# Softmax denominators from four tiles instead of seven, with VectorE adding the first four exponential tiles, and v in three buffers instead of four

## The chip, the cores and the metric

The kernel runs on one core of one Trainium2 chip. The metric is the device time of one execution in microseconds (us), as the median of several runs. Times inside an execution come from a profile of one execution, counted from the start of its span.

The engines are named as the profile names them: PE is TensorE, PEld its weight loads, DVE is VectorE, ACT is ScalarE, POOL is GpSimd, SP is SyncE, which issues DMAs. PSUM is the memory that TensorE writes its sums to; SBUF is the working memory of all engines.

## The reference

An attention over 8 batches, 12 heads, 448 positions and a head size of 64, with q and k normalised, followed by two dense layers with a leaky ReLU between them:

```python
def rmsnorm(x, g):
    return x / np.sqrt(np.mean(x * x, axis=-1, keepdims=True) + 1e-06) * g

q_n, k_n = rmsnorm(q, g_q), rmsnorm(k, g_k)
scores = np.matmul(q_n, k_n.transpose(0, 1, 3, 2)) / np.sqrt(64)
attn = np.exp(scores - scores.max(-1, keepdims=True))
attn = attn / (attn.sum(-1, keepdims=True) + 1e-09)
x = np.matmul(attn, v)                       # (8, 12, 448, 64)
x = x.transpose(0, 2, 1, 3).reshape(3584, 768)
h = x @ w_in                                 # 768 -> 2048
out = np.maximum(0.01 * h, h) @ w_out        # 2048 -> 768
```

The change concerns `attn.sum`, the softmax denominator.

## The kernel before

**Units and tiles.** The attention is cut into 24 units; a unit is four heads of one batch, so a batch has three units (`NQ` is 3). The 448 key positions of a unit are cut into 7 tiles (`NS` is 7) of 64. For tile t, `score` (L195) makes the scores of 64 keys against all 448 queries for the four heads: PSUM tile `sT`, 128 partitions (two heads' keys) by 2 x 448 (two head pairs, index a). `ex` (L214, ScalarE) writes their exponentials to `et[:, t]` in f16, 128 x 896. The sum of `attn.sum` runs over the keys, so over the partitions of each half and over the seven tiles; it is done by matmuls with ones.

**The loop.** From L928 on, unit u is done in one turn of four steps d = 0 to 3, with score tiles (0), (1, 2), (3, 4), (5, 6) (`STEPS`). Instructions are issued in the order in which they stand; each engine executes its own in that order. In step 0, after the scores of tile 0 of unit u, come the leftovers of unit u-1:

- `shift_max(u)` (L232, L234): VectorE takes the maximum over tile 0 and multiplies it into an identity, giving `dg`.
- `pv_slot(u-1)` (L341): TensorE multiplies all seven exponential tiles with v, 28 matmuls of 448 columns.
- `zcol(u-1)` (L283): TensorE sums the exponentials with `onesr`, 16 matmuls on four strips of 32 columns: tiles (0, 1), (6), (2, 3), (4, 5) for each half of the queries (y) and head pair (a). Units 4 to 22 take this path (`narrow`).
- `shift_mm(u)` (L244, L245, L253): TensorE multiplies `dg` with ones, so that the maximum reaches every partition; VectorE reduces it to the bias `eb` of the exponentials of unit u. The matmul comes straight behind `zcol` on TensorE.
- `pv_out(u-1)` (L295) on ScalarE and `zcol_sum(u-1)` (L300) on VectorE clear the two results out of PSUM; `zcol_inv` (L305, L306) forms the reciprocals and copies them by DMA to tile `rz`; `xmul_pool` or `xmul_sb` (L321) multiplies, on POOL or VectorE, into `xts`.

Units 0 to 3 and unit 23 take the older path: `zsum` (L265), 28 matmuls of 448 columns over all seven tiles, and `zinv`.

**What fills the steps.** After its scores and exponentials, each step calls `fill`. It takes items from `queue`: matmul groups of the two dense layers of an earlier batch, which are queued when a batch's units are done: `moe1` (L363), `moe2` (L404), `seven` (L445, a product with seven block multiplications in place of eight, whose extra sums L426 to L435 and PSUM evictions L452, L461 are VectorE's) and in the last batches `late1` (L565). How many items a step takes is worked out from costs written in the code. Behind each item one of the step's `jobs` is issued; what is left of the jobs follows after the last item. An item's evictions are held in `pend` and issued by `flush`, ahead of the next item's matmuls or at the end of the items.

The jobs of a turn prepare later units on VectorE, ScalarE and SP. Step 1: `prep_g(u+1)` (L151), `prep_ssq(u+2)` (L155, two reductions). Step 2: `prep_rinv(u+2)` (L160, L161, ScalarE), `prep_norm(u+2)` (L167, two VectorE products which wait for it), `prep_trd(u+2)` (a transposing DMA on SP, which waits for these). Step 3: `prep_sq(u+3)` (L144, ScalarE).

**v.** `load_v(u)` (L124) is a DMA on POOL's queue into one of `NV` fixed buffers, unit u into buffer u mod `NV`; it waits until the `pv` that read the buffer before has ended. With `NV` 4, the loop issues `load_v(u+3)` in step 0 of turn u.

**Buffers.** `zpool` holds one buffer of each of its tiles (`x32`, `zs`, `rz`), `epool` two of `et`. PSUM has four banks of tag `aux`, which the items, `zcol` and others share, and two double banks `sT`, which the scores and `pv` share.

Of the kernel before, what the change touches and what calls it, by code (L numbers as in the profile page):

```python
# [9 lines left out]
FP16 = mybir.dt.float16  # L10
AF = mybir.ActivationFunctionType
ALU = mybir.AluOpType
# [6 lines left out]
def kernel(  # L19
# [11 lines left out]
    nc = tc.nc  # L31

    B, H, S, D = q.shape
    QH = 4
    NS = 7
    P = 128
    NQ = H // QH
    NU = B * NQ
# [1 line left out]
    KT = DM // P  # L40
    FT = DF // P
    DELTA = 1.0
    NV = 4

    cst = ctx.enter_context(tc.tile_pool(name="cst", bufs=1))
    raws = ctx.enter_context(tc.tile_pool(name="raws", bufs=3))
# [3 lines left out]
    zpool = ctx.enter_context(tc.tile_pool(name="zpool", bufs=1))  # L50
# [6 lines left out]
    def aux(shape, dtype, name):  # L57
        if held:
            return held[0].pop(0)
        return psum.tile(shape, dtype, tag="aux", bufs=4, name=name)  # L60
# [14 lines left out]
    onesr = cst.tile([P, 32], FP16)  # L75
# [12 lines left out]
    gate_t = cst.tile([P, 1], FP16)  # L88
    vts = [cst.tile([P, 2, NS, D], FP16, name=f"vt{i}") for i in range(NV)]
    win16 = cst.tile([P, NQ, 2, DF], FP16)  # L90
# [20 lines left out]
    st = {}  # L111

    def rows(x, u):
        b, g = divmod(u, NQ)
        return x[b, QH * g:QH * g + QH].rearrange("(a r) (p t) d -> (r p) a (t d)", r=2, t=NS)

    def load(u, engines=None):
        raw[u] = [raws.tile([P, 2, NS, D], FP32, tag=name, name=name) for name in ("rq", "rk")]
        st[u] = {}
        for t, src, eng in zip(raw[u], (q, k), engines or (nc.sync, nc.sync)):  # L120
            eng.dma_start(t.rearrange("p a t d -> p a (t d)"), rows(src, u))

    def load_v(u):
        nc.gpsimd.dma_start(vts[u % NV].rearrange("p a t d -> p a (t d)"), rows(v, u))  # L124

# [8 lines left out]
    def buf(u, name):  # L134
        if name not in st[u]:
            shape, dtype, bufs = SHAPES[name]
            st[u][name] = prep_p.tile(shape, dtype, tag=name[:2] if bufs == 3 and name != "qkT" else name, bufs=bufs, name=name)
        return st[u][name]
# [7 lines left out]
    def prep_sqp(u, tis=BOTH):  # L146
        for ti in tis:
            nc.gpsimd.tensor_tensor(buf(u, f"sq{ti}"), raw[u][ti], raw[u][ti], op=ALU.mult)
# [49 lines left out]
    def qk(u, steps):  # L198
        st[u]["sT"] = []
        for t in steps:  # L200
            sT = slot()
            score(u, t, (sT[:, 0], sT[:, 1]))
            st[u]["sT"].append((t, sT))
# [51 lines left out]
    def gate(u):  # L255
        nc.gpsimd.tensor_copy(gate_t, buf(u, "n16")[:, 1, NS - 1, 1, D - 1:D])

    xts = {}

    def zsum(u, t0=0, t1=NS):  # L260
        s = st[u]
        for t in range(t0, t1):
            for r in range(2):
                for a in range(2):
                    nc.tensor.matmul(s["zt"][r][64 * a:64 * a + 64, 0:S], ones16[64 * r:64 * r + 64],  # L265
                                     s["et"][64 * r:64 * r + 64, t, a], start=(t == 0), stop=(t == NS - 1))

    def zsum_slot(u):
        s = st[u]
# [4 lines left out]
    HS = S // 2  # L274

    def zcol(u):
        s = st[u]
        s["zc"] = aux([P, 512], FP32, "zc")
        for i, (t, n) in enumerate(((0, 2), (NS - 1, 1), (2, 2), (4, 2))):
            for y in range(2):  # L280
                for a in range(2):
                    c = 32 * (2 * y + a)
                    nc.tensor.matmul(s["zc"][c:c + 32, 0:n * HS].rearrange("p (k x) -> p k x", k=n), onesr,  # L283
                                     s["et"][:, t:t + n, a, HS * y:HS * y + HS], start=(i == 0), stop=(i == 3))

    def pv_slot(u):
        s = st[u]
        s["pslot"] = slot()
        s["pv"] = [s["pslot"][:, r] for r in range(2)]
        pv(u)  # L290

    def pv_out(u):
        s = st[u]
        s["x32"] = zpool.tile([P, 2, S], FP32, tag="x32", name="x32")
        nc.scalar.copy(s["x32"], s["pslot"][:, :, 0:S])  # L295

    def zcol_sum(u):
        s = st[u]
        s["zs"] = zpool.tile([P, HS], FP32, tag="zs", name="zs")
        nc.vector.tensor_reduce(s["zs"], s["zc"][:, 0:S].rearrange("p (k x) -> p x k", k=2), axis=AXL.X, op=ALU.add)  # L300
        drop(s["zc"])
# [11 lines left out]
    def xmul_sb(u):  # L313
        xmul_pool(u, nc.vector)
# [19 lines left out]
    def pv(u, t0=0, t1=NS):  # L334
# [3 lines left out]
        for t in range(t0, t1):  # L338
            for r in range(2):
                for a in range(2):  # L340
                    nc.tensor.matmul(s["pv"][r][64 * a:64 * a + 64, 0:S], vts[u % NV][64 * r:64 * r + 64, a, t],  # L341
                                     s["et"][64 * r:64 * r + 64, t, a], start=(t == 0), stop=(t == NS - 1))
# [354 lines left out]
    def narrow(u):  # L697
        return 4 <= u < NU - 1
# [46 lines left out]
    with tc.manual_schedule():  # L745
# [108 lines left out]
        load_v(3)  # L854
        load(5)
        prep_sqp(4, (0,))
        load_v(4)
        for f in range(2):
            load_w_out(8 * f, 8)
        qk(1, (2,))  # L860
# [26 lines left out]
        prep_norm(3)  # L887
        load(6)
        gate(3)
        prep_sqp(4, (1,))  # L890
        prep_sqp(5)
        load_v(5)
        qk(2, (2,))
        ex(2)
        trn(3, 0, vcopy)
# [32 lines left out]
        for u in range(3, NU):  # L928
            for d in range(4):
                if d > 0 or u > 3:  # L930
                    qk(u, STEPS[d])
                    if d == 0:
                        shift_max(u)
                        if u == 6:
                            xmul_sb(u - 2)
                        if narrow(u - 1):
                            pv_slot(u - 1)
                            zcol(u - 1)
                            shift_mm(u)
                            pv_out(u - 1)  # L940
                            zcol_sum(u - 1)
                        else:
                            zsum_slot(u - 1)
                            pv(u - 1)
                            shift_mm(u)
                            zinv(u - 1)
                    ex(u)
                jobs = []

                def job(fn, *args):  # L950
                    jobs.append(lambda: fn(*args))

                if d == 0:
                    if u == 3:
                        prep_norm(4)
                        gate(4)
                    elif narrow(u - 1):
                        if u < NU - 1:
                            job(zcol_inv, u - 1)
                    else:  # L960
                        xmul(u - 1)
                    if u + 4 < NU:
                        job(load, u + 4)
                    if u + 3 < NU:
                        load_v(u + 3)
                    if u < 6:
                        prep_sqp(u + 3)
                if d == 1 and narrow(u - 1) and not 5 <= u < 8 and u < NU - 1:
                    xmul_pool(u - 1)
                if u == NU - 1:  # L970
                    if d == 1:
                        job(zcol_inv, u - 1)
                    if d == 2:
                        xmul_pool(u - 1)
                if fed(u, d) and u > 3:
                    push(u // NQ - 1)
                if (u, d) in ((3, 1), (4, 0)):
                    for ti in range(2):
                        prep_tr(u + 1, ti, VV)
                if d == 1 and 5 <= u < NU - 1:  # L980
                    job(prep_g, u + 1)
                if u + 2 < NU:
                    if d == 1:
                        for ti in range(2):
                            job(prep_ssq, u + 2, ALL, (ti,))
                    if d == 2:
                        job(prep_rinv, u + 2)
                        for ti in range(2):
                            job(prep_norm, u + 2, ALL, (ti,))
                        if u > 3:  # L990
                            job(prep_trd, u + 2)
                if d == 1 and 4 <= u < 8:
                    job(weight_sum, u - 4, 0)
                if d == 0 and 5 <= u < 9:
                    job(weight_sum, u - 5, 1)
                if d == 2 and 6 <= u < 8:
                    job(xmul_sb, u - 1)
                if u == NU - 2 and d == 0:
                    for n, tile_ in ((1, (raws, "rq", 3)), (2, (raws, "rk", 3)), (3, None), (4, (prep_p, "sq", 3))):
                        job(win_sum, n, 1, tile_)  # L1000
                    for n in (3, 1, 2, 4):
                        job(x_sum, LATE, n)
                if d == 3 and 6 <= u < NU - 3:
                    for ti in range(2):
                        job(prep_sq, u + 3, ALL, (ti,))
                fill(u, d, jobs)
# [4 lines left out]
        for i, ns in enumerate(((3, 1), (2, 4))):  # L1011
            c, fn = queue[i]
# [33 lines left out]
```

## Time and profile before

| | us |
|---|---|
| median of 3 runs (lowest, highest) | 421.58 (420.45, 421.69) |
| the profiled execution | 420.8 |
| its span in the profile | 419.0 |
| VectorE: `tensor_tensor` 128x512 f16 (L426), mean | 0.42 |
| VectorE: `tensor_tensor` 128x1024 f16 (L426), mean | 0.68 |
| VectorE: `tensor_reduce` 128x896 f32 from PSUM (L232), mean | 1.09 |
| VectorE: norm 128x896 (L167), mean | 1.07 |
| POOL: L321, mean | 2.08 |
| PE: waits for ACT `et` in L195, sum | 3.6 |

Lines of the profile give a start, a duration, the engine, the line of the kernel, the operation with its tiles (out<-in) and how many were merged into one row (x16). A bracket at the end is the idle time of the engine just ahead, and what ended it. Durations of TensorE's matmuls overlap one another; distances between their starts are the better measure. A turn of the loop takes about 12.5 to 19 us, and TensorE is the engine with the least free time.

### The profile page before, as it was taken

To read this page: it belongs to the slowest core of one execution; us is meant where nothing else is said; L and a number is where in the kernel's file an instruction comes from. 1 tells how busy PE (TensorE), PEld (TensorE's weight loads), DVE (VectorE), ACT (ScalarE), POOL (GpSimd) and SP (SyncE) were. 2 spreads that over 40 slices of the span, in tenths; PEclk is the share of its full clock that TensorE was granted. 3 is DMA by queue.
4 is the path that set the end of the run, shared out by engine and by line. 5 is a ranking of instruction groups with operands and counts; after the bars stand their busy time and mean duration, and the time that the engine had idled before them with its cause. 6 is when DMAs were issued, how large, how long until landed. Compare 5 with 4: busy or idle time off the path is not lost.

```text
span 419.0 us, 9148 instructions
## 1 busy us (share of the span) xinstructions
PE 402.7 (96%) x3731; PEld 217.6 (52%) x3731; DVE 279.5 (67%) x459; ACT 304.6 (73%) x474; POOL 82.9 (20%) x75
## 2 busy tenths in 40 slices
PE   7787999999999999999999999999999999999995
PEld 7454444544445544454445544454445547558863
DVE  5888675898569736576449746468349788627762
ACT  5999877768887689867986779967986657653600
POOL 1958422200010121210121111120101101010000
PEclk9999999999999999999999999999999999999999
DMA  8999996889664996677665796578554460032023
GB/s 265 239 251 260 237 252 85 219 153 207 163 153 74 216 229 108 166 177 165 158 127 105 201 193 154 152 147 186 159 111 45 119 152 13 2 82 76 2 54 97
DMA packets 71949, 62.39 MB, mean 149 GB/s; under 512 B 36324, under 2 KB 67044, under 8 KB 71908
## 3 DMA queue, kind: packets, MB, share of 16 engines
q1 hardware_dynamic: 61312, 49.62, 47.2%
q0 software_dynamic: 10272, 11.80, 18.1%
q8 instruction: 29, 0.48, 0.4%
q10 hardware_dynamic: 324, 0.39, 0.3%
q14 instruction: 12, 0.10, 0.1%
HBM read 45.61 MB, written 11.01 MB: 135 GB/s over the span
## 4 chain that ended last, share of the span: by engine, by line
PE 83%; ACT 9%; DVE 6%; issue 1%; DVEq 0%; ACTq 0%
PE hps L363 27%; PE sT L195 8%; PE sT L341 6%; ACT et L214 6%; PE ma L445 5%; PE md L445 5%; PE mc L445 5%; PE bank L445 5%; PE bank L565 4%; PE op L404 3%; PE zc L283 3%; PE mb L445 3%; PE warm L743 2%; PE sT L445 2%; DVE n L167 1%
## 5 line engine op out<-in xcount | busy, mean ns | idle before, releaser
L214 ACT ACTIVATE et<-sT,eb 128x896 f16<-128x896 f32 x166 | 159.5, 1010 | 17.9 <-PE sT L195 16.3
L363 PE MATMUL hps<-xt,win 128*128 128x448 f16 x600 | 120.8, 353 | 0.2 <-DVE xt L350 0.2
L363 PEld LDWEIGHTS <-win 128*128 128x128 f16 x612 | 56.8, 98 | 58.2 <-issue 9.7
L321 POOL TENSOR_TENSOR xt<-x,rz 128x896 f16<-128x896 f32 x16 | 33.2, 2076 | 148.5 <-DMA rz<-zs 117.7
L167 DVE TENSOR_TENSOR n<-rq,rinv 128x896 f16<-128x896 f32 (+2 forms) x25 | 26.7, 1069 | 52.2 <-ACT rinv L161 49.4
L195 PE MATMUL sT<-qkT 64*64 64x448 f16 x664 | 52.4, 363 | 4.7 <-ACT et L214 3.6
L357 ACT ACTIVATE gt<-hps 128x448 f16<-128x448 f32 x100 | 52.4, 549 | 5.4 <-PE hps L363 5.1
L155 DVE TENSOR_REDUCE ssq<-sq 128x14 f32<-128x896 f32 (+2 forms) x49 | 50.3, 1057 | 0.7 <-ACT sq L144 0.7
L445 PEld LDWEIGHTS <-sa 128*128 128x128 f16 x352 | 32.8, 98 | 26.3 <-issue 6.1
L295 ACT COPY x<-sT 128x896 f32<-128x896 f32 x19 | 17.2, 907 | 36.1 <-DVE sT L245 36.1
L124 POOL DMA_DIRECT2D vt<-in_v_dram x24 | 18.2, 758 | 114.5 <-PE sT L341 107.1
L195 PEld LDWEIGHTS <-qkT 64*64 64x64 f16 x672 | 15.5, 104 | 38.0 <-issue 34.6
L445 PEld LDWEIGHTS <-gt 128*128 128x128 f16 x264 | 25.2, 98 | 18.7 <-issue 2.1
L341 PE MATMUL sT<-et,vt 64*64 64x448 f16 x532 | 28.5, 349 | 0.3
L404 PE MATMUL op<-wout,gt 128*128 128x384 f16 x160 | 28.4, 327 | 0.0
L232 DVE TENSOR_REDUCE sT<-sT 128x1 f32<-128x896 f32 x22 | 24.1, 1093 | 5.1 <-PE sT L195 4.9
L341 PEld LDWEIGHTS <-vt 64*64 64x64 f16 x672 | 20.7, 107 | 11.3 <-issue 1.7
L167 DVE TENSOR_TENSOR n<-rk,rinv 128x896 f16<-128x896 f32 (+2 forms) x26 | 26.1, 1010 | 0.0
L404 PEld LDWEIGHTS <-gt 128*128 128x128 f16 x192 | 17.6, 98 | 14.0 <-issue 2.9
L445 PE MATMUL ma<-wout,gt 128*128 128x384 f16 x128 | 23.5, 326 | 0.0
L426 DVE TENSOR_TENSOR sa<-gt 128x512 f16<-128x512 f16 (+1 forms) x15 | 8.1, 542 | 16.0 <-ACT gt L357 12.1
L144 ACT ACTIVATE sq<-rq 128x896 f32<-128x896 f32 (+2 forms) x18 | 16.3, 913 | 1.1 <-DMA rq<-in_q_dram 1.1
(136 smaller groups left out, 522.5 us busy)
## 6 DMA issues: line engine op xcount, KB each, us to landing
rq<-in_q_dram SPq DMA_DIRECT2D x24, 448.0 KB, 4.1
rk<-in_k_dram SPq DMA_DIRECT2D x24, 448.0 KB, 5.6
out_dram<-ost SPq DMA_DIRECT2D x52, 192.0 KB, 2.9
rz<-zs SPq DMA_DIRECT2D x76, 112.0 KB, 2.3
vt<-in_v_dram POOLq DMA_DIRECT2D x24, 224.0 KB, 5.5
win<-in_moe_w_in_dram POOLq DMA_DIRECT2D x8, 384.0 KB, 12.4
wout<-in_moe_w_out_dram POOLq DMA_DIRECT2D x2, 1536.0 KB, 25.6
out_dram<-ost SPq DMA_DIRECT2D x4, 96.0 KB, 2.1
```

Of the source, the lines that this page charges most:

```text
L124: nc.gpsimd.dma_start(vts[u % NV].rearrange("p a t d -> p a (t d)"), rows(v, u))
L155: nc.vector.tensor_reduce(buf(u, "ssq")[:, ti, :, c[0]:c[1]], buf(u, f"sq{ti}")[:, :, c[0]:c[1]], axis=AXL.X, op=ALU.add)
L167: nc.vector.tensor_tensor(buf(u, "n16")[:, ti, c[0]:c[1]].rearrange("p s a d -> p a s d"), src[:, :, c[0]:c[1]], buf(u, "rinv")[:, ti, :, ...
L195: nc.tensor.matmul(banks[a][64 * r:64 * r + 64, 0:S].rearrange("p (t x) -> p t x", t=NS), kT(u, r, a, t), qT(u, r, a), start=True, stop=True)
L214: nc.scalar.activation(s["et"][:, t], sT[:, :, 0:S], AF.Exp, bias=s["eb"], scale=1.0)
L232: nc.vector.tensor_reduce(s["spare"][:, 511:512], sT[:, :, 0:S], axis=AXL.XY, op=ALU.max)
L321: eng.tensor_tensor(xts[b][:, g], s["x32"], s["rz"], op=ALU.mult)
L341: nc.tensor.matmul(s["pv"][r][64 * a:64 * a + 64, 0:S], vts[u % NV][64 * r:64 * r + 64, a, t], s["et"][64 * r:64 * r + 64, t, a], start=(t ...
L357: nc.scalar.activation(dst, src, AF.Prelu, bias=0.0, scale=1.0, alpha=0.01)
L363: nc.tensor.matmul(hps[:, 0:S], win16[:, kt // 2, kt % 2, ts(ft, P)], xt[:, kt // 2, kt % 2], start=(kt == 0), stop=(kt == KT - 1))
L404: nc.tensor.matmul(op2[:, 0:HC], gt[:, ft, ds(col(t), P)], wout16[:, ft, ds(HC * half, HC)], start=(ft == 0), stop=(ft == FT - 1))
L445: nc.tensor.matmul(bank[:, 0:HC], a[:, f], b[:, f], start=(first and f == 0), stop=(f == HF - 1), skip_group_check=not first)
```

## The change

- `acc(u, t)` is new: VectorE adds exponential tile t to a running f16 sum `ea` (128 x 2 x 448, one buffer in `zpool`). The first call (t = 1) adds tiles 0 and 1, the next two add tiles 2 and 3.
- The calls are jobs: t = 1 and t = 2 in step 2, after `prep_rinv` and ahead of `prep_norm`; t = 3 in step 3, ahead of `prep_sq`. Units 4 to 23 have them.
- `zcol` multiplies tiles 4 and 5, then 6, then `ea`: four matmuls each, of 448, 224 and 224 columns, twelve in place of sixteen. Tile 6 goes into one half of the columns and `ea` into the other.
- `zsum` takes `ea` and tiles 4, 5, 6 where a unit has `ea`; among the units of that path, this is unit 23.
- `NV` is 3. The loop issues `load_v(u+2)` in place of `load_v(u+3)`. Ahead of the loop, `load_v(4)` moves from behind `prep_sqp(4, (0,))` to behind `gate(3)`, and `load_v(5)` leaves that part.

```diff
-    NV = 4
+    NV = 3
...
+    NA = 4
+
+    def acc(u, t):
+        s = st[u]
+        if "ea" not in s:
+            s["ea"] = zpool.tile([P, 2, S], FP16, tag="ea", name="ea")
+        nc.vector.tensor_tensor(s["ea"], s["et"][:, 0] if t == 1 else s["ea"], s["et"][:, t], op=ALU.add)
+
+    def ztile(u, t):
+        s = st[u]
+        return s["ea"] if "ea" in s and t < NA else s["et"][:, t]
+
     def zsum(u, t0=0, t1=NS):
         s = st[u]
+        if "ea" in s:
+            t0 = max(t0, NA - 1)
         for t in range(t0, t1):
+            e = ztile(u, t)
...
-                                     s["et"][64 * r:64 * r + 64, t, a], start=(t == 0), stop=(t == NS - 1))
+                                     e[64 * r:64 * r + 64, a], start=(t == 0 or e is s.get("ea")), stop=(t == NS - 1))
...
     def zcol(u):
         s = st[u]
         s["zc"] = aux([P, 512], FP32, "zc")
-        for i, (t, n) in enumerate(((0, 2), (NS - 1, 1), (2, 2), (4, 2))):
+        for k, t in ((-1, NA), (0, NS - 1), (1, 0)):
             for y in range(2):
                 for a in range(2):
                     c = 32 * (2 * y + a)
-                    nc.tensor.matmul(s["zc"][c:c + 32, 0:n * HS].rearrange("p (k x) -> p k x", k=n), onesr,
-                                     s["et"][:, t:t + n, a, HS * y:HS * y + HS], start=(i == 0), stop=(i == 3))
+                    q = slice(HS * y, HS * y + HS)
+                    if k < 0:
+                        nc.tensor.matmul(s["zc"][c:c + 32, 0:S].rearrange("p (k x) -> p k x", k=2), onesr,
+                                         s["et"][:, t:t + 2, a, q], start=True, stop=True, skip_group_check=True)
+                    else:
+                        nc.tensor.matmul(s["zc"][c:c + 32, HS * k:HS * k + HS], onesr, ztile(u, t)[:, a, q],
+                                         start=False, stop=True, skip_group_check=True)
...
         prep_sqp(4, (0,))
-        load_v(4)
...
         gate(3)
+        load_v(4)
         prep_sqp(4, (1,))
         prep_sqp(5)
-        load_v(5)
...
-                    if u + 3 < NU:
-                        load_v(u + 3)
+                    if u + 2 < NU:
+                        load_v(u + 2)
...
                     if d == 2:
                         job(prep_rinv, u + 2)
+                        if u >= 4:
+                            job(acc, u, 1)
+                            job(acc, u, 2)
                         for ti in range(2):
                             job(prep_norm, u + 2, ALL, (ti,))
                         if u > 3:
                             job(prep_trd, u + 2)
+                elif d == 2:
+                    job(acc, u, 1)
+                    job(acc, u, 2)
+                if d == 3 and u >= 4:
+                    job(acc, u, 3)
```

## The prediction

> **What bounds the kernel now.** I read, in this order, the engine shares, the chain of waits, the stretches of two turns, and the order of time around the step from one turn of the unit loop to the next. "Turn n" is the loop pass with u = n; it starts with unit n's first score matmuls.
>
> ```profile
> PE 402.7 (96%) x3731; PEld 217.6 (52%) x3731; DVE 279.5 (67%) x459; ACT 304.6 (73%) x474; POOL 82.9 (20%) x75
> ...
> PE 83%; ACT 9%; DVE 6%; issue 1%; DVEq 0%; ACTq 0%
> ```
> TensorE is busy 96% and holds 83% of the chain, so a shorter TensorE step should count. VectorE has 139.5 us free (419.0 - 279.5); the question is where.
>
> ```profile
> 145.10:159.70 14.60, 14.60 (x129) 6.67 (x128) 7.59 (x11) 12.27 (x21) 2.84 (x2) 1.00 0.88 198
> 208.00:224.60 16.60, 16.60 (x149) 8.19 (x152) 10.85 (x18) 13.56 (x23) 2.84 (x2) 1.00 0.56 124
> ```
> The columns are the stretch, its length, then busy time of PE, weight loads, DVE, ACT, POOL. Turns 10 and 14 leave VectorE 7.0 and 5.75 us. But in turn 14 the free time lies first and the rest is packed. VectorE there, in order of time:
>
> ```profile
> 217.55 0.43 DVE L426 TENSOR_TENSOR sa<-gt 128x512 f16<-128x512 f16 x1 [4.42 <-ACT gt L357]
> ...
> 220.69 0.41 DVE L435 TENSOR_TENSOR sa<-gt,sa 128x512 f16<-128x512 f16 x1
> 221.03 1.08 DVE L167 TENSOR_TENSOR n<-rq,rinv 128x896 f16<-128x896 f32 x1
> 222.03 0.54 DVE L452 TENSOR_TENSOR ost<-mb,ost 128x384 f32<-128x384 f32 x1
> 222.50 1.08 DVE L167 TENSOR_TENSOR n<-rk,rinv 128x896 f16<-128x896 f32 x1
> 223.50 0.54 DVE L452 TENSOR_TENSOR ost<-mc,ost 128x384 f32<-128x384 f32 x1
> 223.96 0.67 DVE L426 TENSOR_TENSOR sa<-gt 128x1024 f16<-128x1024 f16 x1
> 224.65 0.56 DVE L452 TENSOR_TENSOR ost<-md,ost 128x384 f32<-128x384 f32 x1
> 225.13 1.09 DVE L232 TENSOR_REDUCE sT<-sT 128x1 f32<-128x896 f32 x1
> 226.25 0.29 DVE L234 TENSOR_TENSOR dg<-ident,sT 128x128 f16<-128x128 f16 x1
> ```
> TensorE beside it:
>
> ```profile
> 224.54 0.38 PE L195 MATMUL sT<-qkT 64*64 64x448 f16 x4
> 224.76 1.49 PE L341 MATMUL sT<-et,vt 64*64 64x448 f16 x28
> 226.18 0.85 PE L283 MATMUL zc<-et,onesr 128*32 128x448 f16 x16
> 226.96 0.23 PE L244 MATMUL sT<-dg,onesp 128*128 128x64 f16 x2
> ```
> From 217.55 to dg there is no idle VectorE time. The shift matmul L244 needs dg, which ends at 226.54 and is covered by pv (L341) and zc (L283) only until 226.96: a reserve of 0.42 us. Turn 10 is the other kind:
>
> ```profile
> 157.37 1.31 DVE L167 TENSOR_TENSOR n<-rq,rinv 128x896 f16<-128x896 f32 x1 [6.12 <-ACT rinv L161]
> 158.60 1.08 DVE L167 TENSOR_TENSOR n<-rk,rinv 128x896 f16<-128x896 f32 x1
> 160.22 1.10 DVE L232 TENSOR_REDUCE sT<-sT 128x1 f32<-128x896 f32 x1 [0.54 <-PE sT L195]
> ```
> Here VectorE sits idle 6.12 us and again 0.54 us ahead of the maximum.
>
> **What the Trainium skill says.** "VectorE: DVE Perf Modes", section on the perf-mode tiers: a 16-bit `tensor_tensor` in SBUF reaches the doubled rate and no more. The trace agrees: successive f16 adds start 0.33 us apart at 512 columns (207.25, 207.58), 0.60 at 1024 (134.39, 134.99), 0.87 at 1536. "TensorE: Matmul & The Clock Gate", part 3: matmuls on different strips of columns run concurrently. Agrees: 16 column matmuls pass in 0.78 us though each is shown as about 0.35. "SBUF — State Buffer", section on who interferes with whom: a VectorE instruction with two SBUF inputs and a GpSimd one that reads SBUF lock each other out. Agrees: L432 took 0.96 us instead of 0.42 while GpSimd's L321 ran (218.41 to 220.49).
>
> **The change, part by part.** *zc.* Sixteen matmuls (1568 columns per strip: 3 x 448 + 224) become twelve (448 + 224 + 224 = 896), on 19 units. L244 starts 0.78 us after zc starts. By columns at full-size pace (18 matmuls of 448 in 3.50 us, 210.44 to 213.94, so 0.43 ns a column) 672 columns save 0.29; by instruction count 4/16 of 0.78 = 0.20; by columns over the whole 0.78 it would be 0.33. I take 0.28 and keep 0.20 to 0.33. *Last unit's zsum:* 28 matmuls in 1.32 us become 16: 0.56 saved, on the chain.
>
> *The adds.* Three of 128x896 f16 for each of units 4 to 23, 60 in all. Between 0.33 and 0.60 by width: 0.54 each, 1.62 a turn, 32 us in all. Two enter in step 2 ahead of the two L167 norms and the transpose DMA on SP; one in step 3. Behind them on VectorE in order stand the norms, the PSUM evictions of `seven`, and above all shift_max (L232) and dg, for which L244 waits. Only adds that fall into idle time are free.
>
> *v.* NV 3: v of unit u+2 is fetched in turn u rather than u+3, still some 45 us before its pv, and behind the same wait for pv(u-1). At the start, load_v(4) moves behind gate(3) on POOL (35.34 us), after pv(1) has ended (32.7), so its wait costs nothing; the two w_out loads go 0.76 us earlier, the next squares (L148) 0.76 later, ready at 37.7 for a reduce that comes to it at 38.3. load_v(5) moves to turn 3. Cost 0; ends -0.3 and +0.5, as bytes and landing time (5.5 us) stay and the chain holds no DMA.
>
> *Handover by handover.* With reserve S = L244's start minus dg's end, and D the delay of dg, the handover moves by the larger of D + 0.05 - S and -0.28; 0.05 is the smallest distance seen (84.98 to 85.03). S is 0.42 to 0.50, but 0.05 into turns 6 and 8, 0.12-0.13 into 9, 12, 18, and 0.28 into 23.
> - Turn 4: idle 3.47 takes two adds, 0.22 part of the third; D 0.32: -0.12.
> - Turn 5: VectorE is packed from 75.36 to the handover. D 1.62, S 0.05: +1.62.
> - Turn 6: the 1.08 of adds pushes xmul_sb (L321, ends 95.99) past the fifth matmul of the first L363 group, which wants it at 96.17: +0.95, then the handover gains 0.28: +0.67.
> - Turns 7, 11, 17: two adds lie in the wait for rinv; the third is in a packed run: +0.54, +0.47, +0.47.
> - Turns 8, 14, 20: all three in the packed run (turn 8 has 0.20 idle): +1.34, +1.25, +1.25.
> - Turns 9, 12, 18, 21: gaps of 0.32 and 0.61 take half; D about 0.8: +0.45, +0.43, +0.42, +0.40.
> - Turn 15: no second gap, D 1.44, and the first add meets GpSimd's L321 (235.28 to 237.36), 0.52 more: +1.51.
> - Turns 10, 13, 16, 19: hidden: -0.28 each.
> - Turn 22: gaps of 0.56 and 0.16, D 0.92, S 0.28: +0.69.
> - Turn 23: hidden; zsum -0.56.
>
> Gains: 0.12 + 1.12 + 0.56 = 1.80. Losses: 11.5. Net +9.7 us. The profiled execution took 420.8 us (span 419.0), so 430.5 in its own terms; it lay 0.8 below the median, so 431.3 against 421.58.
>
> **Rivals.** *The adds hide everywhere (faster).* VectorE is only 67% busy, and fewer matmuls on a 96% engine is a plain gain: 19 x 0.28 + 0.56 = 5.9, so 415.7. One mechanism decides it, the delay of dg at the handover: up to S - 0.33, about 0.15 us, all is kept, up to S - 0.05 nothing is lost. For it: 139 us idle; against: the runs in turns 5, 8, 14, 20. 0.08.
> *Half hides.* If the waits of the middle turns (7, 9, 11, 12, 17, 18, 21, 22: 3.9 in sum) vanish, because TensorE's stalls let VectorE and ScalarE catch up, +5.8 is left; if the long ones halve too (7.6 to 3.8), +2. 423.5 to 427.4. 0.12.
> *The adds cost more.* Each waits for the one before, as L429 for L426 (0.45 apart against 0.35): 0.1 on some 30 adds, +3; a GpSimd lock in three more turns, 0.5 each, +1.5. 435.8 and up. 0.06.
> *The short matmuls save nothing* (issue-bound): the gains of the quiet handovers go, about +1, within the main case.
>
> **How the numbers follow.** The main case has 0.74, with 427 to 435. The range 425.5 to 435.5 leaves out the faster case (0.08), the lower half of the half-hidden (0.06) and most of the dear one (0.05). A measurement here can't tell less than 0.3% (1.3 us) from no change; 0.03 of the half-hidden case lies there. So faster 0.08, same 0.03, slower 0.89.
>
> **What would show it.** In the profile after: zc from its start to L244 at 0.50 us where L244 doesn't wait; adds of about 0.6 us, x60; DVE near 312 us busy; new waits of PE L244 on DVE dg, 12 or more and some 8 us in sum, longest about 1.6 in turns 5, 8, 14, 15, 20; handovers into 11, 14, 17, 20 without one. The prediction is wrong if L244 waits for dg under 3 us in all, or if the time comes from L445 or L363 waiting on evictions, or from loads.

## The result, and the profile after

The changed kernel takes 433.60 us (median of 4 runs, 433.31 to 435.53), the kernel before 421.58. The ratio is 1.030, 95% interval 1.0267 to 1.0336. In the profiled executions the span grew from 419.0 to 431.9 us, by 12.9.

The engine shares of the changed kernel and the shares of its chain of waits, from the page:

```profile
PE 398.3 (92%) x3643; PEld 216.5 (50%) x3643; DVE 315.5 (73%) x519; ACT 305.1 (71%) x474; POOL 83.0 (19%) x75
...
PE 44%; DVE 25%; ACT 18%; issue 5%; DMA 5%; SPq 2%; DVEq 0%; ACTq 0%
```

TensorE has 4.4 us less work (402.7 before) and yet ends 12.9 us later. VectorE has 36.0 us more, and its share of the chain went from 6% to 25%. The view of TensorE's waits says where (reason, sum in us, times, longest):

```profile
PE sT L244 <- DVE dg L234: 13.7, 12, 1.5
PE sT L195 <- ACT et L214: 3.6, 10, 0.5
...
PE hps L383 <- DVE xt L341: 1.5, 1, 1.5
...
PE bank L585 <- DVE u L598: 0.9, 1, 0.9
PE bank L585 <- DVE v L598: 0.8, 1, 0.8
```

The first line is new: twelve waits of the shift matmul (L244) for `dg`; in each of them L244 starts 0.05 us after `dg` has ended. The second is the 3.6 us of before. The third belongs to turn 6, the last two to turn 22. Turn 14, whose VectorE order the prediction showed, now reads (VectorE, then TensorE):

```profile
227.60 0.61 DVE L266 TENSOR_TENSOR ea<-et 128x896 f16<-128x896 f16 x1
...
228.60 0.61 DVE L266 TENSOR_TENSOR ea<-ea,et 128x896 f16<-128x896 f16 x1
229.13 1.08 DVE L167 TENSOR_TENSOR n<-rq,rinv 128x896 f16<-128x896 f32 x1
...
231.14 0.62 DVE L266 TENSOR_TENSOR ea<-ea,et 128x896 f16<-128x896 f16 x1
...
233.21 1.09 DVE L232 TENSOR_REDUCE sT<-sT 128x1 f32<-128x896 f32 x1
234.33 0.29 DVE L234 TENSOR_TENSOR dg<-ident,sT 128x128 f16<-128x128 f16 x1
```

```profile
231.29 1.49 PE L361 MATMUL sT<-et,vt 64*64 64x448 f16 x28
...
232.92 0.27 PE L303 MATMUL zc<-et,onesr 128*32 128x224 f16 x4
233.01 0.27 PE L303 MATMUL zc<-ea,onesr 128*32 128x224 f16 x4
...
234.67 0.22 PE L244 MATMUL sT<-dg,onesp 128*128 128x64 f16 x2 [1.39 <-DVE dg L234]
```

The sums end sooner (`zc` starts at 232.72 and would release L244 0.50 us later), but `dg` arrives at 234.62, behind three adds. TensorE stands still for 1.39 us.

### The profile page after: what moved, and what is told of

Read it like the earlier page. It is cut to its first block, busy times and chain, and to the rows that moved or that the text cites. A ratio compares the mean times of both kernels' runs of the same rounds, so it can differ in the third digit from the quotient of the medians.

```text
span 431.9 us, 9045 instructions
## 1 busy us (share of the span) xinstructions
PE 398.3 (92%) x3643; PEld 216.5 (50%) x3643; DVE 315.5 (73%) x519; ACT 305.1 (71%) x474; POOL 83.0 (19%) x75
## 4 chain that ended last, share of the span: by engine, by line
PE 44%; DVE 25%; ACT 18%; issue 5%; DMA 5%; SPq 2%; DVEq 0%; ACTq 0%
PE hps L383 16%; ACT et L214 9%; DVE n L167 7%; PE bank L465 5%; ACT gt L377 4%; DVE ea L266 4%; PE sT L195 4%; DMA rq<-in_q_dram 3%; PE bank L585 3%; DVE sT L232 3%; PE sT L361 2%; DVE ost L472 2%; DMA qkT<-n 2%; DVE ssq L155 2%; PE warm L763 2%
## 5 line engine op out<-in xcount | busy, mean ns | idle before, releaser
L214 ACT ACTIVATE et<-sT,eb 128x896 f16<-128x896 f32 x166 | 159.6, 1011 | 17.4 <-PE sT L195 15.7
L383 PE MATMUL hps<-xt,win 128*128 128x448 f16 x600 | 121.0, 353 | 1.8 <-DVE xt L341 1.5
L383 PEld LDWEIGHTS <-win 128*128 128x128 f16 x612 | 56.7, 98 | 59.9 <-issue 11.4
L341 POOL TENSOR_TENSOR xt<-x,rz 128x896 f16<-128x896 f32 x16 | 33.2, 2075 | 150.9 <-DMA rz<-zs 105.3
L124 POOL DMA_DIRECT2D vt<-in_v_dram x24 | 18.2, 758 | 125.3 <-PE sT L361 117.5
L446 DVE TENSOR_TENSOR sa<-gt 128x512 f16<-128x512 f16 (+1 forms) x15 | 8.2, 546 | 26.5 <-ACT gt L377 22.6
L266 DVE TENSOR_TENSOR ea<-ea,et 128x896 f16<-128x896 f16 x40 | 25.9, 647 | 2.2 <-ACT et L214 1.6
```

The source lines that it names most:

```text
L214: nc.scalar.activation(s["et"][:, t], sT[:, :, 0:S], AF.Exp, bias=s["eb"], scale=1.0)
L266: nc.vector.tensor_tensor(s["ea"], s["et"][:, 0] if t == 1 else s["ea"], s["et"][:, t], op=ALU.add)
L341: eng.tensor_tensor(xts[b][:, g], s["x32"], s["rz"], op=ALU.mult)
L383: nc.tensor.matmul(hps[:, 0:S], win16[:, kt // 2, kt % 2, ts(ft, P)], xt[:, kt // 2, kt % 2], start=(kt == 0), stop=(kt == KT - 1))
```

## The experiments

A time is compared with the kernel before on the same chip, 420.8 to 420.9 us in all three groups of runs. The changed kernel was timed in the first comparison alone (433.60 against 421.58), so where a run is set against it, what counts is how much each grew over its own kernel before: 12.0 us in the changed kernel. "The handover into turn n" is the start of L244 in turn n, and its increment is how much the distance from L244 of turn n-1 grew against the kernel before; the increments of a kernel add up to the change of its span. (The prediction counts by the turn left: its "turn 14" is the handover into 15.)

### The parts alone

**v_only**: the kernel before with the buffers and loads of v changed, and nothing else.

```diff
-    NV = 4
+    NV = 3
...
-        load_v(4)
...
+        load_v(4)
...
-        load_v(5)
...
-                    if u + 3 < NU:
-                        load_v(u + 3)
+                    if u + 2 < NU:
+                        load_v(u + 2)
```

> The kernel before with v in three buffers and the moved v loads, no adds and the old sums. Theory (the adds on VectorE delay dg and so the shift matmul): v costs nothing, 421.6 +- 0.6. Rival (part of the loss is the later v loads): some us slower, 423 to 426.

Measured 421.12 us, ratio 1.0003 (0.9992 to 1.0014). The v part costs nothing that can be seen: in its profile every handover from that into 4 on is within 0.01 us of the kernel before.

**matmuls_only**: the short sums without the adds. Tile 3 of the exponentials stands where `ea` stood, so tiles 0 to 2 are missing from the denominators.

```diff
-        return s["ea"] if "ea" in s and t < NA else s["et"][:, t]
+        return s["et"][:, NA - 1] if u >= 4 and t < NA else s["et"][:, t]
...
-                            job(acc, u, 1)
-                            job(acc, u, 2)
```

> The changed kernel without the 60 adds: the short sums read exponential tile 3 where the added tile stood, so tiles 0 to 2 are left out of the denominators of units 4 to 23. Theory: TensorE's saving is real but is cut where dg had next to no reserve before (into turns 6, 8, 9, 12, 18, 23): 13 x 0.28 + 0.45 + 0.56 = 4.7 us less, 416.9. Full saving would be 19 x 0.28 + 0.56 = 5.9, 415.7. Rival (the new matmuls themselves cost: short ones, half-written groups): no faster than 421.

Measured 416.10 us, ratio 0.9879 (0.9862 to 0.9895): 4.8 us gained. Where `dg` comes in time the handover gains 0.28 or 0.29 us (into 7, 11, 13 to 17, 19 to 22; 0.30 into 10), 0.07 to 0.08 where the reserve was small (into 9, 12, 18), and nothing where it was 0.05 us (into 6 and 8); the last unit gains 0.59. So the price of the shorter sums was right, and so was the limit by the reserve. With the span of 413.9 us as the base, the 60 adds of the changed kernel cost 431.9 - 413.9 = 18.0 us, of which the sums pay back 5.1.

**adds_only**: the adds with the old sums over seven tiles, so `ea` is computed and not used.

```diff
-        for k, t in ((-1, NA), (0, NS - 1), (1, 0)):
+        for i, (t, n) in enumerate(((0, 2), (NS - 1, 1), (2, 2), (4, 2))):
```

> The changed kernel with the adds and the three v buffers, but the sums over all seven tiles as before, so that nothing reads the added tile. Theory (where the shift matmul waits for dg, the length of zc in front of it doesn't matter): the twelve handovers that waited stay as late, the others lose their 0.28: about 15.3 us over before, 436.2; the short sums are then worth some 2.5 us beside the adds, against 4.8 alone. Rival (costs and gains add up): 433.6 less base plus 4.9, about 438.

Measured 435.85 us, ratio 1.0369 (1.0329 to 1.0408). Its handovers into 6, 8, 9, 10, 12, 13, 15, 18, 19 and 21 lose what those of the changed kernel lose, within 0.05 us: where `dg` is late, a shorter `zc` only makes TensorE wait longer. (Those into 7, 16, 22 and 23 differ by 0.1 to 0.5.) Beside the adds the short sums are thus worth some 2 us (434.1 - 431.9 = 2.2 in span), not the 5.1 that they are worth alone.

### Adds where VectorE is idle, and where it is not

**packed** (the first `SEL` below): adds only in the 15 turns where the prediction sees no room; the units without adds keep the old sums. **quiet** (the second): adds only in units 10, 13, 16, 19 and 23, where it sees room.

```diff
+    SEL = (4, 5, 6, 7, 8, 9, 11, 12, 14, 15, 17, 18, 20, 21, 22)
+    SEL = (10, 13, 16, 19, 23)
...
-                        if u >= 4:
+                        if u in SEL:
                             job(acc, u, 1)
                             job(acc, u, 2)
```

> The changed kernel with adds and short sums in units 4 to 9, 11, 12, 14, 15, 17, 18, 20, 21 and 22 alone (45 adds), the old sums in 10, 13, 16, 19 and 23. Theory (it counts where the adds fall): all of the loss and none of the gain of the quiet units, about 14.5 us over before, 435.4, so slower than with all 60 adds. Rival (each add costs the same): 45/60 of the adds' cost of some 17.8 us, less the short sums' gain in these units, about 10 over before, 430.8.

> The changed kernel with the adds and the short sums in units 10, 13, 16, 19 and 23 alone (15 adds of 60), the old sums in the others. Theory (it counts where the adds fall): 4 x 0.29 + 0.55 = 1.7 us less than before, 419.9. Rival (each add costs VectorE or its port about the same, 60 adds making 12 us net): a quarter of the loss, about 424.

packed: 435.86 us, ratio 1.0350 (1.0324 to 1.0376). 45 adds lose more than 60 (15.0 us against 12.0), since the 15 others were the ones that paid: the handovers into 11, 14, 17 and 20 and the end give back -0.29, -0.30, -0.29, -0.31 and -0.54 in the changed kernel, 1.7 us in all. That the expected 435.4 was met so closely is in part luck: in the profiled execution the handover into 7 lost 2.53 us instead of 1.41 because TensorE's clock was halved from 86.72 to 90.13 us (last section), while that into 22 lost 0.61 instead of 1.08.

quiet: 419.97 us, ratio 0.9977 (0.9965 to 0.9988), a gain of 0.9 us where 1.7 were expected. The five handovers gained what was expected (-0.29, -0.28, -0.30, -0.29, -0.54), but that into 16, a turn without adds, lost 0.86. GpSimd and VectorE there, in the kernel before and then in quiet:

```profile
235.28 2.08 POOL L321 TENSOR_TENSOR xt<-x,rz 128x896 f16<-128x896 f32 x1 [7.95 <-DMA rz<-zs]
237.12 1.18 DVE L167 TENSOR_TENSOR n<-rq,rinv 128x896 f16<-128x896 f32 x1 [0.32 <-ACT rinv L161]
```

```profile
235.71 2.07 POOL L353 TENSOR_TENSOR xt<-x,rz 128x896 f16<-128x896 f32 x1 [9.26 <-DMA rz<-zs]
236.24 2.49 DVE L167 TENSOR_TENSOR n<-rq,rinv 128x896 f16<-128x896 f32 x1 [0.32 <-ACT rinv L161]
```

The norm takes 2.49 us instead of 1.08 while GpSimd multiplies. The three gains of 0.3 us before it brought the norm forward by 0.88 us, with all the rest of its turn. GpSimd's product, which waits for the DMA of `rz`, came 0.43 us later instead, although that DMA was issued 0.88 us sooner too (229.32 us, 230.20 before). So a transfer that took 1.3 us longer from its issue to the product has laid the product onto the norm; why it took longer isn't shown. The Trainium skill, "SBUF — State Buffer", section on who interferes with whom, says that only VectorE's and GpSimd's shared ports contend, and that this is an exclusive lock; the lines of quiet agree.

**mix**: twelve units, with two adds instead of three in units 4, 7, 8, 11, 14, 17 and 20, and those of 8, 14 and 20 moved forward into step 1, ahead of one of the reductions (there `prep_g` and the other reduction are issued at once and not as jobs).

```diff
+    NAU = {4: 3, 7: 3, 8: 3, 10: 4, 11: 3, 13: 4, 14: 3, 16: 4, 17: 3, 19: 4, 20: 3, 23: 4}
+    EARLY = (8, 14, 20)
```

> Adds only where VectorE has idle time: all three in units 10, 13, 16, 19, 23; the first two (tiles 0 to 2 in the sum, tiles 3 to 6 by matmul, 0.19 us saved) in 4, 7, 11, 17; the same two moved into step 1 ahead of the packed run in 8, 14, 20. Theory: 4 x 0.29 + 0.55 + 7 x 0.19 = 3.0 us less than before, 418.5. Rival (any add costs): slower than the quiet kernel.

Measured 419.35 us, ratio 0.9959 (0.9943 to 0.9974). Units 8, 14 and 20 gain 0.14 to 0.20 each; 7, 11 and 17 lose 0.43, 0.18 and 0.17, although both their adds lie in idle time.

**mix2** leaves 7, 11 and 17 out. **mix_slots** keeps them and puts the first two adds of a turn into the job of `prep_rinv`.

```diff
-                        job(prep_rinv, u + 2)
-                        if u in NAU and u not in EARLY:
-                            job(acc, u, 1)
-                            job(acc, u, 2)
+                        def rinv_acc(u=u):
+                            prep_rinv(u + 2)
+                            if u in NAU and u not in EARLY:
+                                acc(u, 1)
+                                acc(u, 2)
+                        job(rinv_acc)
```

> The mix without units 7, 11 and 17, in which it lost: nine units with adds, the early adds in step 1 for 8, 14 and 20. The sum of what these units measured in the mix: handovers into 9, 15 and 21 -0.19, -0.20, -0.14, into 11, 14, 17 and 20 -0.28 each, the last unit -0.55, so about -2.2 us: 418.7 on a base of 420.9 (ratio 0.9948). Rival (the turns shift against each other and other waits, a lock by GpSimd above all, take the gain): 419.5 to 420, as in the quiet kernel.

> The mix of twelve units, with the same joining of jobs in units 4, 7, 10, 11, 13, 16, 17, 19 and 23. Theory of the slots: the losses into 8, 12 and 18 (+0.43, +0.18, +0.17) become gains of 0.0 to -0.2 each, so 0.8 to 1.2 us less than the mix: 418.3 on a base of 420.9 (ratio 0.9935). Rival (no effect of the place): 419.35, ratio 0.996.

mix_slots: 418.06 us, ratio 0.9941 (0.9926 to 0.9955), the fastest complete kernel of the study, 2.7 us faster than before. The handovers into 8, 12 and 18 went from +0.43, +0.18, +0.17 to -0.01, -0.07, -0.07. mix2: 419.59 us, ratio 0.9970 (0.9958 to 0.9981), so the rival's number: the expected gains are there (-0.19 each into 9, 15 and 21, -0.28 or -0.29 into 11, 14, 17 and 20, -0.59 at the end), and one norm in GpSimd's way takes 1.00 us back at the handover into 18:

```profile
266.03 2.07 POOL L355 TENSOR_TENSOR xt<-x,rz 128x896 f16<-128x896 f32 x1 [8.53 <-DMA rz<-zs]
266.71 2.34 DVE L167 TENSOR_TENSOR n<-rq,rinv 128x896 f16<-128x896 f32 x1 [5.75 <-ACT rinv L161]
```

In the profiled execution of mix_slots the same happens in turn 18 and costs 0.69 us at the handover into 19. In both the norm stands where it stood in the kernel before, 9.8 and 10.1 us after the turn's L244; GpSimd's product is the one that comes later, at 9.14 and 9.42 us instead of 8.03 and 7.56. The profiled execution of mix_slots took 419.47 us, 1.4 above the median of the six, three of which took 417.8 to 417.9. Perhaps the two met in some executions only; the other five were not traced, so this isn't shown.

### Attempts to take the waits away with all 60 adds

**slots**: the same joining of jobs in the changed kernel.

> All 60 adds, but the first two of a turn are issued in the same job as prep_rinv, so that they take no job slots of their own and the norms stand behind the same items as in the kernel before. Theory (in turns 7, 11 and 17 the adds took the slots, and the norms came to stand behind s1, which waits for ScalarE's gt): the handovers into 7, 11 and 17 fall from +1.41, +0.73, +0.73 to about +0.54, +0.47, +0.47, so 1.4 us less than the changed kernel: 432.2 against a base of 421.6 (ratio 1.025). Rival (the place of the norms is indifferent, VectorE simply has 1.62 us more to do per turn): 433.6, ratio 1.029 to 1.030.

One correction to this text: turn 7's own loss is the handover into 8 (+0.97), and the +1.41 it names belongs to turn 6. So the drop to expect was 0.95 us, not 1.4. Measured, the handovers into 8, 12 and 18 fell to +0.53, +0.46 and +0.47, as the theory of the slots has it. But the whole took 436.02 us, ratio 1.0362 (1.0346 to 1.0379), a growth of 15.2 us and not of 12.0 (the profiled spans differ by 1.6), since the handovers into 15 and 21 rose from +1.18 and +1.16 to +3.52 and +2.07. Turn 14 of slots, GpSimd, VectorE and TensorE:

```profile
224.37 2.08 POOL L341 TENSOR_TENSOR xt<-x,rz 128x896 f16<-128x896 f32 x1 [7.41 <-ACT et L214]
```

```profile
225.28 1.65 DVE L266 TENSOR_TENSOR ea<-et 128x896 f16<-128x896 f16 x1
226.96 0.63 DVE L266 TENSOR_TENSOR ea<-ea,et 128x896 f16<-128x896 f16 x1
227.50 0.55 DVE L481 COPY ost<-ma 128x384 f32<-128x384 f32 x1
```

```profile
224.57 1.46 PE L465 MATMUL mb<-tw,sa 128*128 128x384 f16 x8
228.10 2.14 PE L465 MATMUL ma<-wout,gt 128*128 128x384 f16 x8 [2.07 <-DVE ost L481]
```

The adds now stand ahead of an eviction (L481) that TensorE wants from 226.03 on (224.57 + 1.46), and the first of them is locked by GpSimd until 226.45. TensorE starts at 228.10, after 2.07 us. Turn 20 repeats this with a wait of 2.20 us; that the handover into 15 lost 1.45 us more than that into 21 goes with TensorE's clock, halved from 228.74 to 232.15 us (last section). What was won for the norms was lost, with more, on an eviction.

**cover**: one item of the dense layers is put between `zcol` and the shift matmul in turns 6 to 21, so that TensorE has work while `dg` is late. **cover_mid**: the same in turns 12 to 18.

```diff
                             zcol(u - 1)
+                            if 6 <= u <= 21 and queue:
+                                c, fn = queue.pop(0)
+                                fn()
+                                debt[0] -= c
                             shift_mm(u)
```

> The changed kernel with one item of the dense layers (1.1 to 1.3 us of matmuls) taken out of the queue between zc and the shift matmul in turns 6 to 21; the same work in another order. Theory (the loss is TensorE standing at the shift matmul until dg is there): the eleven waits in these turns, 12.2 us in sum, shrink to under 3, and the time falls by 6 to 10 us to 424 to 428; the exponentials of the turn start up to 1.2 us later, which may take some of it back on ScalarE. Rival (VectorE as a whole, or its evictions, is the bound): no gain, 433.

> All 60 adds, and one item of the dense layers between zcol and the shift matmul in turns 12 to 18 only. In these turns the changed kernel loses 3.6 us, waiting 5.3 us for dg. Theory (the cover removes the wait for dg, but the bias and so the exponentials come later, and TensorE waits for ScalarE in L195 in its place): 432.5, between 431.8 and 433.4 on a base of 421.6 (ratio 1.024 to 1.028). Rival (the wait is really covered, and the earlier cover kernel lost its gain only at the start and the end, with the halved clock): 429, ratio 1.018.

cover: 435.08 us, ratio 1.0340 (1.0306 to 1.0375); cover_mid: 435.96 us, ratio 1.0354 (1.0341 to 1.0367). Their growth is 14.2 and 15.2 us, no less than that of the changed kernel. Neither theory's number was met, and the expected gain of cover did not come. The waits of TensorE in cover:

```profile
PE sT L195 <- ACT et L214: 5.7, 16, 0.5
PE sT L244 <- DVE dg L234: 4.1, 7, 0.9
PE sT L195 <- ACT x L315: 2.4, 3, 1.9
...
PE bank L585 <- ACT gt L595: 1.5, 1, 1.5
```

The wait for `dg` fell from 13.7 to 4.1 us, but the bias `eb` comes later, and the waits for ScalarE grew by 6.0 us (5.7 + 2.4 + 1.5 against 3.6). That is one part. Another is the lock. For each kernel I took the VectorE instructions that lasted over 0.25 us longer than the median of their shape: 3.0 us of excess in 5 instructions in the kernel before, 6.5 in 8 in the changed one, but 15.7 in 17 in cover, 13.3 in 14 in cover_mid and 13.2 in 13 in slots. All of them overlap a product of GpSimd: L341 (L321 in the kernel before), or its squares (L148) for two that all five kernels have (near 63 and 79 us, 0.7 each). A third part is the clock, below. The item that is moved is also missing from a later step, which shifts the places of the jobs; this wasn't tested apart. How the sum of cover splits among these wasn't settled.

### The adds on GpSimd

**pool_adds**: `nc.gpsimd.tensor_tensor` instead of `nc.vector.tensor_tensor` in `acc`.

```diff
-        nc.vector.tensor_tensor(s["ea"], s["et"][:, 0] if t == 1 else s["ea"], s["et"][:, t], op=ALU.add)
+        nc.gpsimd.tensor_tensor(s["ea"], s["et"][:, 0] if t == 1 else s["ea"], s["et"][:, t], op=ALU.add)
```

> The changed kernel with the 60 adds on GpSimd instead of VectorE. Theory: shift_max no longer stands behind adds, but each add takes some 2 us there, reads SBUF and locks out VectorE's instructions with two SBUF inputs (norms, the block sums), and the third one may come too late for zc: gains at the handovers are given back in norms of 2 us and more and in zc waiting for ea; between 425 and 440, open. If the lock were no matter and ea in time: near 417.

Measured 494.76 us, ratio 1.1766 (1.1709 to 1.1823), outside of every expectation. Groups of instructions of pool_adds by form (busy us, mean ns of one):

```profile
L266 POOL TENSOR_TENSOR ea<-ea,et 128x896 f16<-128x896 f16 x40 | 92.0, 2299 | 3.1
L167 DVE TENSOR_TENSOR n<-rk,rinv 128x896 f16<-128x896 f32 x22 | 45.7, 2077 | 0.0
```

An add takes 2.0 to 2.3 us there against 0.62 on VectorE, and the second norm on VectorE takes 2.08 us instead of 1.08. `dg` came no sooner (L244 waited 24.6 us), and `zc` waited 18.2 us for `ea`. TensorE's clock was halved ten times between 89 and 452 us as well, so the loss isn't that of the adds' place alone.

## Why the prediction was right, step by step

The direction, the mechanism and the range were right; the sum was 3.2 us short of the span's growth (9.7 against 12.9), 2.3 short of the medians' (12.0). Fifteen of the twenty handovers came within 0.3 us; of the five others four were too cheap and one too dear, so the sum does not owe its place in the range to errors that cancel. By handover:

| turn left | predicted | measured | | turn left | predicted | measured |
|---|---|---|---|---|---|---|
| 4 | -0.12 | -0.16 | | 14 | +1.25 | +1.18 |
| 5 | +1.62 | +1.79 | | 15 | +1.51 | +0.95 |
| 6 | +0.67 | +1.41 | | 16 | -0.28 | -0.29 |
| 7 | +0.54 | +0.97 | | 17 | +0.47 | +0.73 |
| 8 | +1.34 | +1.16 | | 18 | +0.42 | +0.62 |
| 9 | +0.45 | +0.60 | | 19 | -0.28 | -0.31 |
| 10 | -0.28 | -0.29 | | 20 | +1.25 | +1.16 |
| 11 | +0.47 | +0.73 | | 21 | +0.40 | +1.08 |
| 12 | +0.43 | +0.62 | | 22 | +0.69 | +1.79 |
| 13 | -0.28 | -0.30 | | 23 | -0.56 | -0.54 |

- **zc and zsum**: right. `zc` to L244 is 0.50 us where L244 doesn't wait (167.11 to 167.61), 0.78 before.
- **The adds' duration**: right, 0.62 us, and the next independent instruction 0.53 later. The "dependency" of the rival is real for two adds next to each other: 0.71 to 0.72 from start to start (95.09 to 95.81), not 0.54. But only five pairs of the changed kernel stand so. VectorE's busy time came to 315.5 us instead of 312; three adds that met GpSimd account for 3.4 of it (0.78, 1.53 and, in turn 23 where it cost nothing, 1.12).
- **v at cost 0**: right (v_only).
- **Quiet turns 10, 13, 16, 19, and 23**: right within 0.03 us.
- **Packed turns 5, 8, 14, 20**: right within 0.2 us. **Turn 15**: too dear, as the lock it foresaw did not occur: GpSimd's product came 7.65 us after the turn's L244 and not 8.28 as before, and ended at 244.42, when the first add began. In adds_only it came at 8.45, an add took 1.28 us, and the handover lost 1.32.
- **Turn 6**, the term "pushes xmul_sb 1.08": mis-sized. The wait of L383 for it is 1.53 us, not 0.95. VectorE of the changed kernel there:

```profile
91.40 0.45 DVE L151 TENSOR_SCALAR qkT<-qkT,gcol 128x896 f16<-128x896 f16 x1 [0.47 <-DMA qkT<-n]
...
95.09 0.61 DVE L266 TENSOR_TENSOR ea<-et 128x896 f16<-128x896 f16 x1
95.81 0.63 DVE L266 TENSOR_TENSOR ea<-ea,et 128x896 f16<-128x896 f16 x1
```

  The transposing DMA of the norms, which the adds of turn 5 had delayed, holds up VectorE for 0.47, which it did not before, and the two adds take 1.26. The prediction counted the DMA as something behind the adds, but not VectorE behind the DMA a turn later.
- **Turns 7, 11, 17**, "two adds lie in the wait for rinv": wrong in the order of instructions, and slots and mix_slots show it. Each add takes one of the job slots behind the items, so the norms are issued an item later, behind `s1` (L446):

```profile
108.35 0.63 DVE L266 TENSOR_TENSOR ea<-ea,et 128x896 f16<-128x896 f16 x1 [0.27 <-ACT et L214]
112.36 0.43 DVE L446 TENSOR_TENSOR sa<-gt 128x512 f16<-128x512 f16 x1 [3.38 <-ACT gt L377]
112.82 0.42 DVE L449 TENSOR_TENSOR sa<-sa,gt 128x512 f16<-128x512 f16 x1
113.16 1.08 DVE L167 TENSOR_TENSOR n<-rq,rinv 128x896 f16<-128x896 f32 x1
```

  Here `s1` waits until 112.36 for ScalarE's `gt`, and the norm stands behind it. In slots it starts at 111.86, ahead of `s1`, and the handover falls by the 0.44 us that were missing.
- **Turns 21 and 22**, "gaps take the rest": 0.68 and 1.10 us too cheap. In both the first add ran into GpSimd's product. In turn 21 the product came 8.56 us after the turn's L244, and 7.48 in the kernel before; in adds_only and packed it came at 7.5 again, met no add, and the handover lost 0.61, so 0.47 of the 1.08 are the lock. In turn 22, where no run without a lock is at hand:

```profile
358.95 2.08 POOL L341 TENSOR_TENSOR xt<-x,rz 128x896 f16<-128x896 f32 x1 [14.91 <-ACT gt L377]
359.36 2.15 DVE L266 TENSOR_TENSOR ea<-et 128x896 f16<-128x896 f16 x1
```

  and TensorE's L585 then waits 0.92 and 0.80 us for `u` and `v`. This is the half of "the adds cost more" that did occur, in two other turns than turn 15 and at 0.78 and 1.53 us of excess instead of 0.52.
- **Turns 9, 12, 18**: 0.15 to 0.20 too cheap. In turn 12 the three adds filled 0.71 of the 0.92 us of gaps; an eviction behind the first add waited 0.21 for its matmuls.
- **Waits of L244 for `dg`**: twelve as expected, 13.7 us in sum instead of about 8. The 8 does not follow from the prediction's own list, whose losses at these twelve handovers add up to 10.2; they measured 11.6. At eleven of them the wait contains, besides the loss, some 0.2 us by which `zc` ends sooner for nothing; at that into 6 TensorE had waited 0.4 us for `ea` already.

The likeliest rival, that half of it hides, did not occur: the changed kernel's own handovers show no catching up, and in packed those into 9, 10, 12, 13, 15, 16 and 18 lose the same within 0.04 us, although four of the turns among them were relieved of their adds.

## What to carry to other kernels

An engine that is 67% busy can be full just where it matters: count the new work against the reserve ahead of the one instruction that the bound engine waits for, turn by turn, and make the change only in the turns that have room (here twelve units of twenty and two or three adds each: a gain of 2.7 us, against a loss of 12.0 for all). A new piece of work also takes a place in the queue of issue; look at what is pushed behind an instruction with a long wait. Where GpSimd and VectorE both work on SBUF, a transfer that lands 1 to 2 us later than in another execution can lay a product of one onto an instruction of the other, which cost 0.7 to 1.0 us at a handover here. So the gain of a small change has to be read by handover, not from the total alone.

## What the runs showed of the hardware

- **TensorE's clock was halved after some waits and not after others, and the length of the wait alone doesn't tell which.** In slots it was after the wait of 2.07 us ahead of 228.10, and not after that of 2.20 ahead of 329.40. In each trace the halved stretches last 3.41 us (6.83 where two join; the one at the very end is cut short or longer), and their starts lie whole multiples of 3.41 us apart. Cut at these points, slots reads so (stretch, its length, busy us of PE, weight loads, DVE, ACT, POOL, then the granted clock):

```profile
225.32:228.74 3.42, 1.35 (x9) 0.68 (x8) 3.39 (x7) 0.54 (x2) 1.12 (x1) 1.00 0.46 177
228.74:232.15 3.41, 3.41 (x18) 1.21 (x16) 2.98 (x4) 1.82 (x3) 0.00 (x0) 0.50 0.03 5
327.72:331.14 3.42, 1.74 (x16) 0.82 (x15) 3.38 (x7) 0.24 (x1) 0.01 (x1) 1.00 0.00 0
331.14:334.55 3.41, 3.41 (x36) 1.86 (x32) 3.39 (x6) 3.41 (x5) 0.00 (x0) 1.00 0.25 49
```

  The longer wait began 0.52 us ahead of a cut, so less of it fell into one stretch. All fourteen traces agree from 40 us on: a stretch at full clock in which TensorE was busy for 1.54 us or less was followed by a halved one, a stretch with 1.74 us or more was not, and of two between (1.58 and 1.59) one was. (In the first 40 us some with up to 2.0 us busy were.) So a wait of 1.52 us ahead of 86.29 was enough in packed, and one of 1.52 us ahead of 86.66 was not in the changed kernel, where the busy time of the stretch was 1.54 and 2.25 us. While the clock was halved, eight matmuls took 2.14 us instead of 1.46 (slots, 228.10), and sixteen 4.45 instead of 2.77 (cover, 89.99). The Trainium skill, "TensorE: Matmul & The Clock Gate", Part 1, gives half rate after at least one idle window of some 3.4 us; the length agrees, but here the stretch need not be idle throughout.
- **A VectorE instruction with two inputs in SBUF that starts during a product of GpSimd ends a fixed time after that product.** For the adds it is 0.48 us (turn 22 above: 361.51 against 361.03), for the norms 0.95 (quiet: 238.73 against 237.78), so they took up to 2.51 us (slots) and 2.99 us (cover). An eviction, which reads PSUM, ran at its usual 0.56 us within the product of turn 21 (342.65, the product from 341.96 to 344.03). It holds the other way round too: in slots a product that started 0.02 us after an add, at 143.82, took 2.52 us instead of 2.08.
